# The hole between two SBUF pools, 160 bytes in place of 192

## Chip, cores and metric

One core of a Trainium2 chip runs the kernel. The metric is the device time of one execution in microseconds, the median over runs.

## What is computed

Three stages follow each other: a linear attention with decay (retention), a gated feed-forward layer (SiLU) with RMS norm, and a second layer whose activation is a softmax times its input with a layer norm. All is float32.

```python
for t in range(S):                        # S = 768, 4 batches, 8 heads of 64
    state = gamma * state + einsum('bhd,bhe->bhde', k[:, :, t], v[:, :, t])
    y[:, :, t] = scale * einsum('bhd,bhde->bhe', q[:, :, t], state)

xn = x / rms * rms_g                      # x: 3072 tokens x 512
g = xn @ w_gate; val = xn @ w_val         # 512 x 1536 each
x2 = (g * sigmoid(g) * val) @ w_out       # 1536 x 512

h = x2 @ w_in                             # 512 x 1024
e = exp(h - max(h)); sm = e / (sum(e) + 1e-9)
solu = h * sm
out = ((solu - mean) / sqrt(var + 1e-6) * g_ln) @ w_out2   # 1024 x 512
```

## The kernel before

The 3072 tokens are six blocks of 512. The weights come as 64-bit words and are turned to float32 on the way in. Every float32 product is three TensorE matmuls: both factors are split into a high and a low part (split, line 99: ACT copies the high part to float32r, VectorE or GpSimd subtracts it for the low part), and mm3 (lines 805 to 808) adds high times high, high times low, low times high into one PSUM bank. A matmul has a moving operand (rhs, at most 128x512 here) and weights (lhsT, 128x128), which TensorE loads by an instruction of its own ahead of each matmul. In the profile the name at the left of a pair is the moving operand: X<-r,wo streams r past weights from wo.

bc_block(n) walks the twelve slices m of the inner dimension (1536 = 12 x 128). Each step has a burst into bank GB (gate) and one into VB (value), twelve matmuls with xnh and xnl streaming past a weight tile w, and a burst of twelve into X0 to X3, where the gated product (r, its two parts) streams past the tile wo of the step before. In block 0 the weights are made from the raw input. Tiles of even slices are then w4 and wo (profile names w and wo), tiles of odd slices lie in CV. All are stored to DRAM (scr) and loaded again for later blocks. Blocks 2 to 5 run the second layer by de_quarters: seven products of half matrices in place of eight, at line 1180, each six matmuls of 128x512, for two halves t, with w2ih, w2il, xnh, xnl or T1 (a w4 tile) streaming past parts in r and x; then e_mm, where w2oh and w2ol stream past the transposed r. Blocks 0 and 1 use d_mm and e_mm alone, with x as weights and w2ih, w2il streaming. Block 5 runs the gate and value products in the seven-product form too, on 256 columns (seven_mm, line 913; profile line 918), with B11, B21, B22 in xnh and xnl and T1 to T4 in tiles rq, rk, kd and qd.

Between these bursts stand pieces of the attention for the next block (64 and 128 columns, lines 119 and 180) and transposes (line 1048). Their places are set by slot numbers that are written out by hand (slot, w_slot, at). Loads go through SyncE's queue in program order, stores of weights and results through ACT's.

SBUF holds two pools. A pool lays its tiles one behind the other, a tag with several buffers taking as many places, in the order in which the tags first occur; the second pool begins where the first ends. spacer(n, name) allocates n bytes in a partition that nothing uses, in the first pool; gap(name, n) does it in the second. In bytes of a partition, the built program has:

| tiles | pool | starts, modulo 512 |
|---|---|---|
| QK and w2ih, KV and w2il, xT, xnh, xnl, U, ssq, w2oh, CV and w2ol | cp, first | 448 |
| mtab 32, qtab 32, ones 192, ident 224, smaller tables elsewhere | cp | as said |
| x2 (x), r2 (r), f4 (f), st, sq, w4 (w), wo, rv, A | wp, second | 480 |
| rq, rk, kd, qd, first sm | wp, behind a gap | 384 |

The first pool begins at 16,512; the spacer of 320 bytes at line 64 puts QK at 16,832 = 32 x 512 + 448, and all large tiles behind it are multiples of 512 bytes long. The last tile of the first pool ends at 121,120; the spacer of 192 bytes at line 1321 puts the second pool's first tile, x2, at 121,312 = 236 x 512 + 480. A gap of 416 bytes ahead of rq and another ahead of kd leave these at 384, one of 96 bytes ahead of rv and one of 352 ahead of A bring these to 480 again.

Of the kernel before, what the change touches and what calls it, by code (L numbers as in the profile page):

```python
# [42 lines left out]
def retention_moe_kernel(ctx: ExitStack, tc: tile.TileContext, qk0, q2, kt, kv, wpk, w2i, w2o,  # L43
# [17 lines left out]
    def spacer(n, name):  # L61
        cp.tile([P, n // 4], F32, tag=name, name=name)
# [1255 lines left out]
    make_identity(nc, ident)  # L1318
    mhalf = cp.tile([P, 16], F32, tag="mhalf", name="mhalf")
    nc.gpsimd.memset(mhalf, -0.5)  # L1320
    spacer(192, "sp1")
    nc.gpsimd.memset(U0, 0.0)
    for t in U:
        nc.gpsimd.memset(t, 0.0)
# [192 lines left out]
```

## Time and profile before

| | |
|---|---|
| median of 3 runs | 995.77 us (995.46 to 1001.24) |
| profiled execution | 997.89 us, its span 996.1 us |
| granted TensorE clock, mean over the span | 0.99 |
| TensorE busy, matmuls | 973.9 us, 98% |
| VectorE, ScalarE, GpSimd busy | 517.4, 408.4, 449.3 us |
| DMA | 231.95 MB, 233 GB/s in the mean |

How to read it: the busy time of TensorE counts a matmul from its start to a modelled end, and successive matmuls overlap, so that 128x512 matmuls that start about 230 ns apart each last about 395 ns. A stretch can be 100% busy and yet have shorter or longer steps in it. The step, from one start to the next, is read from the timeline, in which neighbours of the same line and names are merged (x2, x6) and others stand on rows of their own.

### The profile page before, as it was taken

How to read it: one execution, taken by the hardware profiler on the slowest of the kernel's cores; microseconds unless marked ns; L12 is line 12 of the kernel's file. 1: busy time of each engine (PE TensorE's matmuls, PEld its weight loads, DVE VectorE, ACT ScalarE, POOL GpSimd, SP SyncE). 2: the span in 40 equal slices, each digit the busy share in tenths (PEclk: the TensorE clock that was granted, in tenths of full speed). 3: DMA queues.
4: the chain of work that ended last, by engine and by line, in shares of the span. 5: the costliest groups of instructions: out<-in, count | busy, mean ns of one | idle time of the engine just before them, and what ended most of it. 6: DMA issues, size and time to landing. Idle time of an engine off the chain costs nothing.

```text
span 996.1 us, 17723 instructions
## 1 busy us (share of the span) xinstructions
PE 973.9 (98%) x6636; PEld 798.8 (80%) x6636; DVE 517.4 (52%) x1040; ACT 408.4 (41%) x792; POOL 449.3 (45%) x494
## 2 busy tenths in 40 slices
PE   7999998999999999999999999999999999999998
PEld 7877787888787887888777888778788888899987
DVE  3787765463365754334574422566422457334474
ACT  2767655583244343322355221246312246321354
POOL 5886855582043395533537424527333425300022
PEclk8799999999999999999999999999999999999999
DMA  9689998996513315989943799861688954698501
GB/s 341 215 319 391 356 308 320 344 355 220 205 53 97 96 43 171 308 270 296 317 122 115 247 356 322 279 215 57 211 319 310 331 196 138 208 329 298 190 1 43
DMA packets 101334, 231.95 MB, mean 233 GB/s; under 512 B 13184, under 2 KB 43264, under 8 KB 100224
## 3 DMA queue, kind: packets, MB, share of 16 engines
q1 hardware_dynamic: 92464, 205.64, 60.5%
q10 hardware_dynamic: 8784, 25.17, 6.5%
q8 instruction: 53, 0.87, 0.3%
q14 instruction: 33, 0.27, 0.1%
HBM read 188.82 MB, written 41.94 MB: 232 GB/s over the span
## 4 chain that ended last, share of the span: by engine, by line
PE 86%; DMA 6%; POOL 3%; ACT 2%; DVE 1%; issue 1%; SPq 1%; ACTq 0%; POOLq 0%; DVEq 0%
PE X L806 10%; PE X L807 10%; PE X L808 10%; PE GB L806 7%; PE GB L808 7%; PE GB L807 7%; PE VB L806 6%; PE VB L807 6%; PE VB L808 6%; DMA wo<-scr 3%; PE X L1180 3%; PE YB L119 2%; PE VB L918 2%; PE X L1048 2%; PE YB L918 2%; PE VB L1180 2%
## 5 line engine op out<-in xcount | busy, mean ns | idle before, releaser
L825 DVE TENSOR_TENSOR f<-VB,f 128x512 f32<-128x512 f32 x60 | 41.4, 690 | 146.5 <-PE VB L808 128.7
L807 PE MATMUL X<-r,wo 128*128 128x512 f32 x260 | 102.5, 394 | 0.0
L806 PE MATMUL X<-r,wo 128*128 128x512 f32 x260 | 98.9, 395 | 3.1 <-DMA wo<-scr 3.1
L808 PE MATMUL X<-r,wo 128*128 128x512 f32 x260 | 101.5, 390 | 0.0
L854 ACT ACTIVATE f<-GB 128x512 f32<-128x512 f32 x60 | 35.7, 595 | 148.4 <-PE GB L808 148.3
L707 POOL TENSOR_TENSOR st<-st,x 128x512 int32<-128x512 int32 x52 | 70.2, 1352 | 55.7 <-ACT x L704 13.0
L100 ACT CAST r<-f 128x512 fp32r<-128x512 f32 x72 | 44.6, 619 | 121.8 <-DVE f L825 103.4
L806 PE MATMUL GB<-xnh,w 128*128 128x512 f32 (+1 forms) x220 | 88.0, 400 | 2.5 <-ACT f L854 1.1
L807 PE MATMUL GB<-xnl,w 128*128 128x512 f32 (+1 forms) x220 | 87.6, 398 | 2.1 <-DVE xnl L101 2.0
L806 PE MATMUL VB<-xnh,w 128*128 128x512 f32 (+1 forms) x220 | 87.1, 396 | 0.0
L808 PE MATMUL GB<-xnh,w 128*128 128x512 f32 (+1 forms) x220 | 87.1, 396 | 0.0
L808 PE MATMUL VB<-xnh,w 128*128 128x512 f32 (+1 forms) x220 | 86.7, 394 | 0.2 <-POOL w L101 0.2
L807 PE MATMUL VB<-xnl,w 128*128 128x512 f32 (+1 forms) x220 | 86.6, 394 | 0.0
L101 DVE TENSOR_TENSOR r<-f,r 128x512 fp32r<-128x512 f32 x72 | 61.0, 849 | 29.3 <-ACT r L100 28.7
L602 POOL TENSOR_TENSOR x<-x 128x512 f32<-128x512 f32 x24 | 31.6, 1320 | 92.1 <-DMA x<-scr 63.0
L291 POOL TENSOR_TENSOR U<-U,u 128x256 f32<-128x256 f32 x27 | 17.4, 645 | 98.8 <-PE SB L119 59.4
L806 PEld LDWEIGHTS X<-r,wo 128*128 128x128 f32 x260 | 48.7, 188 | 14.2 <-issue 3.3
L101 POOL TENSOR_TENSOR r<-st,r 128x512 fp32r<-128x512 f32 x8 | 10.3, 1288 | 110.2 <-ACT r L100 110.2
L806 PE MATMUL X<-w2oh,r 128*128 128x512 f32 (+1 forms) x144 | 57.6, 400 | 1.3 <-ACT r L1051 0.8
L808 PEld LDWEIGHTS X<-r,wo 128*128 128x128 f32 x260 | 48.8, 188 | 10.6
L807 PEld LDWEIGHTS X<-r,wo 128*128 128x128 f32 x260 | 48.8, 188 | 10.3 <-issue 0.2
L808 PE MATMUL X<-w2oh,r 128*128 128x512 f32 (+1 forms) x144 | 56.3, 391 | 0.0
(458 smaller groups left out, 2540.2 us busy)
## 6 DMA issues: line engine op xcount, KB each, us to landing
w<-scr SPq DMA_DIRECT2D x96, 512.0 KB, 5.7
wo<-scr SPq DMA_DIRECT2D x59, 512.0 KB, 5.2
x<-in_wpk SPq DMA_DIRECT2D x36, 512.0 KB, 6.0
x<-scr SPq DMA_DIRECT2D x25, 512.0 KB, 6.3
sscr<-x SPq DMA_DIRECT2D x24, 512.0 KB, 8.3
scr<-CV ACTq DMA_DIRECT2D x18, 512.0 KB, 6.0
rv<-in_kv SPq DMA_DIRECT2D x128, 64.0 KB, 2.3
scr<-w ACTq DMA_DIRECT2D x12, 512.0 KB, 5.2
```

Of the source, the lines that this page charges most:

```text
L100: h = nc.scalar.copy(hi, src)
L101: (lo_eng or nc.vector).tensor_tensor(out=lo, in0=src, in1=hi.bitcast(F32), op=ALU.subtract)
L119: return lambda: nc.tensor.matmul(out, lhsT=lhsT, rhs=rhs, start=start, stop=stop)
L602: nc.gpsimd.tensor_tensor(out=w[:, 0, :], in0=w[:, 0, :], in1=w[:, 1, :], op=ALU.add)
L707: nc.gpsimd.tensor_tensor(out=ti, in0=ti, in1=lo, op=ALU.add)
L806: nc.tensor.matmul(ps, lhsT=lh, rhs=rh, start=start, stop=False)
L807: nc.tensor.matmul(ps, lhsT=lh, rhs=rl, start=False, stop=False)
L808: return nc.tensor.matmul(ps, lhsT=ll, rhs=rh, start=False, stop=stop)
L825: recent["dve"] = nc.vector.tensor_tensor(out=a, in0=GV[1], in1=silu[:, 0, :], op=ALU.mult)
L854: recent["act"] = nc.scalar.activation(s[:, 0, :], GV[0], AF.Silu)
L918: nc.tensor.matmul(ps, lhsT=x, rhs=y[:, k, :], start=start and k + i == 0, stop=k == 1 and i == 2, skip_group_check=True)
L1180: last["mm"] = nc.tensor.matmul(bank, lhsT=x[:, k, ts_], rhs=y[:, k, :], start=start and k + i == 0, stop=k == 1 and i == 2, skip_group_ch ...
```

## The change

The spacer at line 1321, the last thing that the first pool allocates, has 160 bytes in place of 192.

```diff
     mhalf = cp.tile([P, 16], F32, tag="mhalf", name="mhalf")
     nc.gpsimd.memset(mhalf, -0.5)
-    spacer(192, "sp1")
+    spacer(160, "sp1")
     nc.gpsimd.memset(U0, 0.0)
```

No instruction of any engine stands at another place, in the order of the built program, and none has another shape. All tiles of the second pool start 32 bytes lower: those at 480 modulo 512 are at 448 then, those at 384 at 352. The first pool's tiles stay.

## Rows read from the trace of the kernel before

**Rows 1.** The page, busy time of each engine; then the chain that ended last.

```profile
PE 973.9 (98%) x6636; PEld 798.8 (80%) x6636; DVE 517.4 (52%) x1040; ACT 408.4 (41%) x792; POOL 449.3 (45%) x494
...
PE 86%; DMA 6%; POOL 3%; ACT 2%; DVE 1%; issue 1%; SPq 1%; ACTq 0%; POOLq 0%; DVEq 0%
```

**Rows 2.** Windows: length, busy us (instructions) by engine, granted clock, DMA share, GB/s.

```profile
0.00:75.00 75.00, 66.51 (x495) 56.95 (x496) 50.29 (x77) 41.67 (x81) 56.29 (x61) 0.89 0.82 292
75.00:165.00 90.00, 86.95 (x461) 69.43 (x459) 66.20 (x103) 56.72 (x98) 61.96 (x57) 1.00 0.95 336
```

**Rows 3.** Waits of TensorE: line, who was waited for, us in all, times, longest.

```profile
PE X L806 <- DMA wo<-scr: 3.1, 2, 1.8
...
PE X L1180 <- POOL r L101: 1.2, 1, 1.2
```

**Rows 4.** Timeline of TensorE, 98 to 104 us: start, length (us), line, out<-in, shapes.

```profile
98.23 0.39 PE L807 MATMUL X<-r,wo 128*128 128x512 f32 x1
...
100.50 0.39 PE L808 MATMUL X<-r,wo 128*128 128x512 f32 x1
100.72 0.40 PE L806 MATMUL GB<-xnh,w 128*128 128x512 f32 x1
...
103.29 0.40 PE L808 MATMUL GB<-xnh,w 128*128 128x512 f32 x1
```

**Rows 5.** Timeline of TensorE, 87 to 98 us, block 0, an odd weight tile.

```profile
87.19 0.40 PE L806 MATMUL X<-r,CV 128*128 128x512 f32 x1
...
89.76 0.40 PE L808 MATMUL X<-r,CV 128*128 128x512 f32 x1
...
91.69 0.39 PE L808 MATMUL GB<-xnh,CV 128*128 128x512 f32 x1
...
92.85 0.39 PE L807 MATMUL GB<-xnl,CV 128*128 128x512 f32 x1
...
95.80 0.39 PE L808 MATMUL VB<-xnh,CV 128*128 128x512 f32 x1
```

**Rows 6.** Groups of TensorE by line and shape: count, busy us, mean ns, idle.

```profile
L807 PE MATMUL X<-r,wo 128*128 128x512 f32 x260 | 102.5, 394 | 0.0
...
L806 PE MATMUL GB<-xnh,w 128*128 128x512 f32 x212 | 85.1, 401 | 2.1 <-ACT f L854 1.1 <-ACT xnh L100 1.0
...
L806 PE MATMUL X<-w2oh,r 128*128 128x512 f32 x136 | 55.3, 407 | 1.3 <-ACT r L1051 0.8 <-ACT f L1088 0.6
...
L808 PE MATMUL GB<-w2oh,r 128*128 128x512 f32 x48 | 19.3, 403 | 0.0
...
L806 PE MATMUL X<-w2ih,x 128*128 128x512 f32 x40 | 16.0, 400 | 0.0
...
L808 PE MATMUL X<-r,CV 128*128 128x512 f32 x24 | 9.6, 399 | 0.0
...
L808 PE MATMUL VB<-w2ih,x 128*128 128x512 f32 x16 | 6.3, 396 | 0.0
```

**Rows 7.** Timeline of TensorE, last block, 128x256 matmuls, six in a row.

```profile
878.15 0.87 PE L918 MATMUL YB<-qd,A 128*128 128x256 f32 x6
878.86 0.29 PE L918 MATMUL GB<-xnh,w 128*128 128x256 f32 x1
```

**Rows 8.** The page, DMA issues: out<-in, queue, count, KB each, median us to landing.

```profile
scr<-CV ACTq DMA_DIRECT2D x18, 512.0 KB, 6.0
...
scr<-w ACTq DMA_DIRECT2D x12, 512.0 KB, 5.2
```

**Rows 9.** Chain that ended last, in order of time: start, length (us), what.

```profile
485.23 11.55 DMA wo<-scr
...
649.38 11.17 DMA wo<-scr
```

**Rows 10.** Windows of TensorE alone, around the granted clock's fall at 166 us.

```profile
163.00:166.00 3.00, 1.03 (x4) 1.00 1.01 392
...
166.30:169.70 3.40, 3.40 (x10) 0.50 1.02 411
```

## The prediction

> **What bounds the kernel now.** I read four views, in this order. The page's first part and its chain say whose work sets the end: TensorE is busy 98% of the span and the chain of work that ended last runs 86% of its way over TensorE's lines, 6% over DMA, 3% over GpSimd [rows 1]. The windows say where that does not hold: up to 75 us TensorE is busy 66.5 of 75 us, and from 75 to 165 us it is busy 87 of 90 us while the DMA engines are at 0.95 [rows 2]. After that the waits of TensorE are single events of 1 to 2 us [rows 3]. So from 165 us on, and over most of 75 to 165 us, time is the number of matmuls times the step from one matmul's start to the next. A busy time of 98% does not say that this step is as short as it can be, so the third view is the timeline of TensorE, read for starts, and the fourth the groups by line and shape, read for counts.
>
> In the timeline, look at two bursts that follow each other without a gap. From 98.23 to 100.50 us ten steps of X<-r,wo (128x512) take 2.27 us: **227.0 ns** each. From 100.72 to 103.29 us eleven steps of GB<-xnh,w, the same shape, take 2.57 us: **233.6 ns** each [rows 4]. Same clock, same columns, no wait. What differs is where the operands lie. r, x, w, wo and f are tiles of the second pool, which begin at byte 480 modulo 512; xnh, xnl, CV and w2 are tiles of the first, at 448. While r streams, the weights fetched for the next matmul come from wo: 480 and 480. While xnh streams, they come from w: 448 and 480.
>
> The trace holds both cross cases, in block 0, where odd weight tiles live in CV. X<-r,CV (480 streaming, 448 weights) makes eleven steps from 87.19 to 89.76 us: 233.6 ns. GB<-xnh,CV and VB<-xnh,CV (448 and 448) make thirteen steps from 92.85 to 95.80 us: 226.9 ns [rows 5]. So r is fast with wo and slow with CV, xnh is fast with CV and slow with w. No tile is slow by itself. **Equal start bytes: 227; 32 bytes apart, in either direction: 233.6.** The difference is 6.6 ns.
>
> **What the change does.** It shortens a hole of 192 bytes to 160. No instruction is added, removed or moved on any engine. Every tile of the second pool starts 32 bytes lower: 480 becomes 448, and the few at 384 (rq, rk, kd, qd, sm) go to 352.
>
> *Matmuls that become equal.* From the groups [rows 6], 128x512 matmuls with 448 against 480: the six groups with xnh or xnl and w, 212 each, 1,272; the three with w2oh or w2ol and r into X, 136 each, 408, and into GB, 48 each, 144; the three with w2ih or w2il and x into X, 40 each, 120, and into VB, 16 each, 48; the three X<-r,CV, 24 each, 72. Line 1180 has seven products of six matmuls for two t in four blocks, 336, all mixed but the product with T1 (48): 288. Together 2,352. At 6.6 ns that is **15.5 us**.
>
> *Matmuls that are equal already* (X<-r,wo 780, the xn,CV groups 144, T1 48) keep their operands equal, since both move, or neither. But they are not always at 227: after an interruption the first five steps are slower. From 91.69 to 92.85 us, right behind an attention piece, five steps take 1.16 us, 232.0 ns each [rows 5]. An interrupted burst of equal operands so pays 5 times 5, 25 ns. Today nearly all of the 60 bursts of line 806 to 808 into X pay it, since the burst before them is mixed. After the change that is gone (60 times 25 ns, 1.5 us gained), and instead every stretch behind an interruption pays it: some 56 attention pieces and 48 groups of transposes, about 104 times 25 ns, 2.6 us lost. Net: 15.5 + 1.5 - 2.6 = **14.4 us**.
>
> *The 128x256 matmuls* of the last block step at 118 ns, six in 0.71 us, with A and w weights alike [rows 7]; all of them are mixed today (448 or 384 against 480), so the trace has no equal case of this shape. Three of seven products become equal, 216 matmuls; T1 to T4 stay 96 bytes apart. Below, nothing; above, the whole 6.6 ns, 1.4 us. Since stretches of six or twelve lie between mixed ones and would mostly be first steps, I take 0.2 us.
>
> *What shifts without a price.* The fp32 matmuls of the attention and the transposes have 64 or 128 columns; most pairs keep their distance (rq and rk 0, rv and kd 96), qd against U goes from 64 to 96 bytes, ident against f from 256 to 224: nothing, since no row gives a sign either way. DMAs now begin at 448. Stores that begin there already (scr<-CV) land in 6.0 us, those from 480 (scr<-w) in 5.2 us [rows 8]. The CV stores lie in the busiest stretch, so I take nothing; the bound is 0.8 us a transfer. TensorE waited 3.1 us in all for weights from DMA [rows 3], so that is where a later landing would show.
>
> *What does not reach the end.* Before 75 us TensorE is not the bound: about 50 mixed matmuls lie there, 0.3 us lost. From 75 to 165 us about 200 do, 1.3 us; at a DMA share of 0.95 I count half as lost, 0.7 us. The two longest transfers on the chain, 11.55 and 11.17 us of wo<-scr [rows 9], are fixed lengths that a faster TensorE overtakes: 22.7 us at 14.4 in 830 us is 0.4 us. The waits that end on another engine or a DMA [rows 3] grow where TensorE comes early: 1.7 us, by choice; for scale, those on wo<-scr and on GpSimd's r are 3.1 and 1.2 us now, 4.3 together. What is late next is therefore wo<-scr and the chain of GpSimd's r at line 101. Sum: 14.4 + 0.2 - 0.3 - 0.7 - 0.4 - 1.7 = **11.5 us**.
>
> The profiled execution took 997.89 us, 1.8 us more than its span of 996.1; the median is 995.77, so the profiled one stands 2.1 us (0.2%) above it, and the gain is taken from the median: 995.77 - 11.5 = **984.3 us**.
>
> **Rivals.**
>
> *The fast step does not hold (0.15).* If the many interruptions keep TensorE in the first-steps pace of 232.0 ns, the gain is 1.6 ns times 2,352, 3.8 us, of which the 3.1 us above do not arrive: 995 us. Half way between that and the forecast's 14.4 us stands 9.1 - 3.1 = 6.0 us, 990 us, which I take for this case, since some bursts are long. For it: X<-r,wo bursts start slow each time. Against it: thirteen steps at 226.9 in one go [rows 5].
>
> *Nothing changes (0.11).* The steps would belong to something other than the distance of the two operands, and moving both leaves them: 995.8 us. Against it stand the crossed pairs [rows 5]; for it, that w2 against r and x is seen mixed only, over a third of the count.
> [...]
>
> *Slower, by the clock (0.04).* [...]
>
> **How the numbers follow.** The forecast has 0.70: 984.3, of itself between 980.5 (14.4 us and the 256-column bound of 1.4 us, 0.5 us lost) and 987.4 (losses twice as large, 14.6 - 6.2 = 8.4 us). The range 980.5 to 991 takes in that and the upper half of the first rival and leaves out no change, slower and the rest of the first rival, about 0.2. About 1% is what a measurement of this kernel can tell from no change, here 10 us, so 985.8 us. The forecast lies 1.5 us below that bound; I give four fifths of its 0.70 to faster, 0.57; the remainder with the first two rivals is 0.39; slower 0.04.
>
> **What would show it.** In the profile after: GB<-xnh,w and GB<-w2oh,r step at 227 ns in long bursts; X<-r,wo right behind them has no slow first steps; TensorE's waits on wo<-scr and on GpSimd's r grow by 1 to 2 us together; counts and order are the same. If the w2 groups stay at 233.6 the gain is a third smaller. If all steps are 227 and the end moves less than 8 us, the time went into waits, and the waits' view will name them. If the steps are still mixed, the cause is not the distance.

## The result

The kernel with the hole of 160 bytes takes 988.28 us (median of 8 runs, 983.88 to 992.16) against 996.77 us before (8 runs): ratio 0.9908, 95% interval 0.9881 to 0.9935, 8.5 us less. Three further comparisons in the experiments below put the same two kernels side by side: 0.9890 (0.9861 to 0.9919), 0.9903 (0.9866 to 0.9939) and 0.9888 (0.9860 to 0.9917), which are 11 to 12 us each. The profiled execution took 983.88 us, its span is 982.1.

The page after, busy times and the chain by engine, beside [rows 1]:

```profile
PE 958.7 (98%) x6636; PEld 797.5 (81%) x6636; DVE 518.8 (53%) x1040; ACT 408.7 (42%) x792; POOL 448.8 (46%) x494
...
PE 74%; POOL 7%; DMA 6%; DVE 5%; ACT 3%; issue 3%; SPq 2%; ACTq 0%; POOLq 0%; DVEq 0%
```

TensorE is busy 15.2 us less with the same 6,636 matmuls, and all other engines are busy as long as before, within 2 us. The share is 98% in both: it did not show that there was something to gain, and does not show that it was gained.

The timeline of TensorE after, block 1, the first matmul of five bursts that follow each other (start, length, line, pair):

```profile
184.52 0.39 PE L806 MATMUL X<-r,wo 128*128 128x512 f32 x1
...
187.24 0.39 PE L806 MATMUL GB<-xnh,w 128*128 128x512 f32 x1
...
189.96 0.39 PE L806 MATMUL VB<-xnh,w 128*128 128x512 f32 x1
...
192.68 0.39 PE L806 MATMUL X<-r,wo 128*128 128x512 f32 x1
...
195.40 0.39 PE L806 MATMUL GB<-xnh,w 128*128 128x512 f32 x1
```

Each burst of twelve takes 2.72 us, 226.7 ns a matmul. GB<-xnh,w, 233.6 ns in [rows 4], now has the step of X<-r,wo, and X<-r,wo directly behind VB starts at the fast step at once. The products with w2, which the trace before shows with unequal starts only, moved too. GB<-w2oh,r, first and last matmul of a burst of twelve, before and then after:

```profile
294.69 0.40 PE L806 MATMUL GB<-w2oh,r 128*128 128x512 f32 x1
...
297.26 0.40 PE L808 MATMUL GB<-w2oh,r 128*128 128x512 f32 x1
```

```profile
288.41 0.39 PE L806 MATMUL GB<-w2oh,r 128*128 128x512 f32 x1
...
290.90 0.39 PE L808 MATMUL GB<-w2oh,r 128*128 128x512 f32 x1
```

Eleven steps take 2.57 us before, 233.6 ns each, and 2.49 us after, 226.4 ns each.

The waits of TensorE after, beside [rows 3]:

```profile
PE X L806 <- DMA wo<-scr: 5.3, 2, 3.1
...
PE X L1180 <- POOL r L101: 1.0, 1, 1.0
```

The wait on wo<-scr is 5.3 us in this profile, 3.1 us in the one before. That a faster TensorE made it longer is not shown: with the slow step it is 5.5 us in run d64 and 4.3 us in run d128 below. The longer of its two events, and what the clock did behind it (timeline, then windows of TensorE alone: length, busy us, granted clock, DMA share, GB/s):

```profile
479.15 0.77 PE L806 MATMUL X<-r,wo 128*128 128x512 f32 x1 [3.08 <-DMA wo<-scr]
```

```profile
476.00:478.90 2.90, 0.06 (x5) 1.00 1.02 407
478.90:482.30 3.40, 3.15 (x8) 0.50 1.02 425
```

TensorE is idle for almost all of 476.0 to 478.9 us, then the granted clock is 0.50 for 3.4 us, in which matmuls of 128x512 step at 426 ns (five steps from 479.71 to 481.84 us). There is no such stretch at this place in the profile before, but there is a longer one in d64.

### The profile page after: what moved, and what is told of

It is laid out like the page before. It is cut to its first block, busy times and chain, and to the rows that moved or that the text cites. A ratio compares the mean times of both kernels' runs of the same rounds, so it can differ in the third digit from the quotient of the medians.

```text
span 982.1 us, 17723 instructions
## 1 busy us (share of the span) xinstructions
PE 958.7 (98%) x6636; PEld 797.5 (81%) x6636; DVE 518.8 (53%) x1040; ACT 408.7 (42%) x792; POOL 448.8 (46%) x494
## 4 chain that ended last, share of the span: by engine, by line
PE 74%; POOL 7%; DMA 6%; DVE 5%; ACT 3%; issue 3%; SPq 2%; ACTq 0%; POOLq 0%; DVEq 0%
PE X L806 9%; PE X L807 9%; PE X L808 9%; PE GB L806 6%; PE GB L808 6%; PE GB L807 6%; PE VB L806 5%; PE VB L807 5%; PE VB L808 5%; DMA wo<-scr 3%; PE X L1180 3%; PE VB L1180 2%; PE YB L119 2%; PE GB L1180 2%; PE VB L918 2%
## 5 line engine op out<-in xcount | busy, mean ns | idle before, releaser
L806 PE MATMUL GB<-xnh,w 128*128 128x512 f32 (+1 forms) x220 | 86.4, 393 | 2.3 <-ACT f L854 1.1
L808 PE MATMUL GB<-xnh,w 128*128 128x512 f32 (+1 forms) x220 | 85.7, 390 | 0.1
L806 PE MATMUL VB<-xnh,w 128*128 128x512 f32 (+1 forms) x220 | 85.6, 389 | 0.0
L808 PE MATMUL VB<-xnh,w 128*128 128x512 f32 (+1 forms) x220 | 85.1, 387 | 0.3 <-POOL w L101 0.3
L808 PEld LDWEIGHTS X<-r,wo 128*128 128x128 f32 x260 | 49.1, 189 | 10.2
```

Of the source, the lines that this page charges most:

```text
L806: nc.tensor.matmul(ps, lhsT=lh, rhs=rh, start=start, stop=False)
L808: return nc.tensor.matmul(ps, lhsT=ll, rhs=rh, start=False, stop=stop)
```

## Where the gain arises and where it is lost

The first 400 matmuls of 128x512 lie in block 0 and the weights' conversion. The one after them is the first X<-r,CV behind the seam of block 0. Its row before, after, and in a later profile of the changed kernel (run again3):

```profile
165.77 1.04 PE L806 MATMUL X<-r,CV 128*128 128x512 f32 x3
```

```profile
162.59 0.63 PE L806 MATMUL X<-r,CV 128*128 128x512 f32 x1
```

```profile
163.48 1.05 PE L806 MATMUL X<-r,CV 128*128 128x512 f32 x2
```

From there to the end of the span is 996.1 - 165.8 = 830.3 us before, 982.1 - 162.6 = 819.5 after and 981.2 - 163.5 = 817.7 us in the later profile: **10.8 and 12.6 us** less. The three microseconds ahead of this row are hardly the change's work. The first 128x512 matmul of the program starts at 48.0 us in the profile before and at 44.1 to 46.2 us in four profiles of the changed kernel; but in run d64 below, where the slow step is kept, it starts at 43.85 us. The stretches of half clock in the first 45 us lie at other places in one profile than in another (from 9.3 and 33.2 us before, from 28.3 us after); that they set this start is not shown.

Part of the 10.8 and 12.6 us is still the place of a stretch at half clock. It lies wholly behind the row before (166.3 to 169.7 us, [rows 10]) and in part ahead of it after (161.4 to 164.9 us). The 421st matmul of 128x512 stands behind that stretch in every profile, at 171.98 us before and 168.20 us after. From there to the end of the span it is 10.2 us less in the profile after, and 11.5, 11.1 and 11.7 us less in three later profiles of the changed kernel (again, again2, again3).

Ahead of 165 us the change brought nothing: the lead of the changed profile is 3.9 us at the first 128x512 matmul and 3.8 us at the 421st. Behind 165 us it grows evenly, about 0.7 us for 140 matmuls, to 9.5 us at 459 us; at the seam with the wait above it falls to 7.3 us, grows again, and is 13.4 us near the end. (These leads are differences of start times of the same matmul in the two timelines.)

## Experiments

**Both pools at 480 (eq480).** Equal starts at the other place.

```diff
-    spacer(320, "sp0")
+    spacer(352, "sp0")
...
-    spacer(192, "sp1")
+    spacer(160, "sp1")
```

> The first spacer has 352 bytes in place of 320, the second 160: both pools' large tiles start at 480 modulo 512, as the second pool's did in the kernel before, and the distance is 0 as in the changed kernel. Theory 1 (the distance between moving operand and weights sets the step): GB<-xnh,w and GB<-w2oh,r step at 227 ns, TensorE's busy time 957 to 962 us, time 984 to 992. Theory 2 (the second pool's own place counts, 448 being a multiple of 64 and 480 not, for TensorE or for DMA): steps of 233 ns as in the kernel before, time 994 to 999.

984.11 us, span 982.3; the kernel before took 995.50 us beside it. One run each, here and for the next three distances. Timeline of TensorE, first matmul of four bursts:

```profile
201.50 0.39 PE L806 MATMUL X<-r,wo 128*128 128x512 f32 x1
...
204.22 0.39 PE L806 MATMUL GB<-xnh,w 128*128 128x512 f32 x1
...
206.94 0.39 PE L806 MATMUL VB<-xnh,w 128*128 128x512 f32 x1
...
209.66 0.39 PE L806 MATMUL X<-r,wo 128*128 128x512 f32 x1
```

2.72 us a burst again, with both at 480 as with both at 448: of these two places neither counts, the distance does. A share of the DMAs in the gain by where the second pool's tiles begin is excluded with it, since here that pool lies as in the kernel before. From the 421st matmul to the end it is 10.7 us less than before.

**Distances of 64, 128 and 256 bytes (d64, d128, d256).** The two spacers have 288 and 224, 224 and 288, 96 and 416 bytes in place of 320 and 192.

> Spacers of 288 and 224 bytes: the first pool at 416, the second at 480, 64 bytes apart. If only equal start bytes modulo 512 give the fast step: 233 ns in the mixed groups, time 994 to 999. If equality modulo 64 is enough: 227 ns, 984 to 992. X<-r,wo, within one pool, keeps 227 in either case.

998.28 us, span 996.5. Timeline, four bursts:

```profile
204.56 0.39 PE L806 MATMUL GB<-xnh,w 128*128 128x512 f32 x1
...
207.36 0.39 PE L806 MATMUL VB<-xnh,w 128*128 128x512 f32 x1
...
210.16 0.39 PE L806 MATMUL X<-r,wo 128*128 128x512 f32 x1
...
212.90 0.39 PE L806 MATMUL GB<-xnh,w 128*128 128x512 f32 x1
```

Mixed bursts take 2.80 us, 233.3 ns a matmul; X<-r,wo, within one pool, 2.74 us, of which the first steps are the slow ones. One group lies between: X<-r,CV, in which the second pool's tile streams past weights of the first, steps at 230.6 ns (59 steps).

The same profile shows that the wait on wo<-scr and the fall of the clock behind it also come with the slow step (waits of TensorE from 200 to 960 us, then a window of TensorE alone):

```profile
PE X L806 <- DMA wo<-scr: 5.5, 3, 3.5
```

```profile
485.80:492.60 6.80, 6.08 (x15) 0.50 1.01 415
```

Up to this place the profile of d64 runs level with the one before, 3.6 us ahead at the 421st matmul and 3.7 us at 459 us; behind it, it is 1.4 us late.

> Spacers of 224 and 288 bytes: 352 and 480, 128 bytes apart. Equality modulo 512 alone: 233 ns, 994 to 999 us. Equality modulo 64 or 128: 227 ns, 984 to 992.

998.40 us, span 996.6. Timeline, three bursts:

```profile
208.76 0.40 PE L806 MATMUL GB<-xnh,w 128*128 128x512 f32 x1
...
211.56 0.40 PE L806 MATMUL VB<-xnh,w 128*128 128x512 f32 x1
...
214.36 0.39 PE L806 MATMUL X<-r,wo 128*128 128x512 f32 x1
```

2.80 us for mixed bursts.

> Spacers of 96 and 416 bytes: 224 and 480, 256 bytes apart. Equality modulo 512 alone: 233 ns, 994 to 999 us. Equality modulo 64, 128 or 256: 227 ns, 984 to 992.

985.16 us, span 983.4. Timeline, four bursts:

```profile
203.35 0.39 PE L806 MATMUL X<-r,wo 128*128 128x512 f32 x1
...
206.07 0.39 PE L806 MATMUL GB<-xnh,w 128*128 128x512 f32 x1
...
208.79 0.39 PE L806 MATMUL VB<-xnh,w 128*128 128x512 f32 x1
...
211.51 0.39 PE L806 MATMUL X<-r,wo 128*128 128x512 f32 x1
```

2.72 us, as with a distance of 0. So what counts, as far as these five distances show it, is the distance **modulo 256**, not 512: 0 and 256 are fast, 32, 64 and 128 are slow, in these bursts by about the same 6.6 ns. From the 421st matmul to the end d256 takes 11.5 us less than the profile before, d128 0.2 us less, and d64, with its long stretch at half clock, 4.0 us more. The modulus that the change aimed at is wider than needed.

**All pairs equal (alleq).**

```diff
-        gap("gq", 416)
+        gap("gq", 512)
...
-        gap("gr", 96)
+        gap("gr", 0)
...
-            gap("gd", 416)
+            gap("gd", 512)
...
-        gap("ga", 352)
+        gap("ga", 256)
...
     ones = cp.tile([P, P], F32, tag="ones", name="ones")
     nc.vector.memset(ones, 1.0)
+    ident = cp.tile([P, P], F32, tag="ident", name="ident")
```

(A gap of 0 allocates nothing; ident is no longer allocated further down.)

> The changed kernel with the gaps of the second pool set to 512, 0, 512 and 256 bytes, so that rq, rk, kd and qd too begin at 448 modulo 512, and with ident ahead of a small table, at 192 (448 modulo 256). All pairs of the attention, the transposes and all products of the last block are then equal modulo 256. Theory 1 (equal starts help every shape): 128x256 products with T1 to T4, now 117 ns, and the 64- and 128-column matmuls step faster by up to 6 ns, busy time of TensorE down by 2 to 4 us. Theory 2 (the gain belongs to 512 columns; at 256 equal pairs step at 120 ns, mixed ones at 117): T1 to T4 go from 117 to 120 ns, busy time up by 0.5 to 1 us.

987.62 us (one run); TensorE's busy time is 962.0 us against 958.7 to 960.8 in four profiles of the changed kernel. The last block in the changed kernel (equal products with xnh and xnl, then one with T4 in qd, mixed, six in a row; the eleven steps run from the first row's start to the second's):

```profile
879.00 0.28 PE L918 MATMUL SB<-xnl,x 128*128 128x256 f32 x1
...
880.32 0.87 PE L918 MATMUL YB<-qd,A 128*128 128x256 f32 x6
881.02 0.28 PE L918 MATMUL GB<-xnh,x 128*128 128x256 f32 x1
```

and in alleq, where the products with T2 and T3 in rq and rk are equal too:

```profile
884.93 0.88 PE L918 MATMUL GB<-rq,x 128*128 128x256 f32 x6
885.65 0.88 PE L918 MATMUL VB<-rk,x 128*128 128x256 f32 x6
886.37 0.88 PE L918 MATMUL VB<-kd,x 128*128 128x256 f32 x6
```

In these bursts of 256 columns equal pairs step at 120.0 ns (eleven steps in 1.32 us in the changed kernel, six in 0.72 in alleq), mixed ones at 116.7 (six in 0.70 us). Over all 274 steps of the products with T1 to T4 the mean is 117.8 ns in the changed kernel and 119.9 in alleq. Equal is the slower of the two there, by 2 to 3 ns. The transposes and the attention's matmuls did not move: steps of 64 columns have a mean of 15.2 ns in both, the transposes with 128 columns 112.3 and 112.4 ns. Theory 2 holds for the steps: the gain belongs to 512 columns. The busy time rose by more than its 0.5 to 1 us, but the profiles of the changed kernel differ by 2.1 us among themselves.

**The changed kernel again (again, again2, again3).**

> The changed kernel itself, for its spread and beside the next two. Its runs so far spread over 8 us, with granted clocks of 0.984 to 0.991, the kernel before over 3 us. Theory 1 (in some runs TensorE's waits on wo<-scr at the seams are followed by stretches at half clock, as at 478.9 us of its profile): median 986 to 990, lower clocks in the longer runs. Theory 2 (the spread came from single bad runs): all runs within 2 us, 983 to 986.

987.65 us (984.98 to 991.02), before 999.09 us (994.57 to 1004.18, 17 runs), ratio 0.9890. Theory 1 holds for the median, but not as it was meant: the kernel before spreads as widely, over 10 us, and its long runs too have the lower granted clock (0.986 in the longest, 0.993 in the shortest). So the spread isn't brought by the change.

> The changed kernel once more, on the chip of the run before it: the step of 227 ns and the waits on wo<-scr as before; ratio to the kernel before between 0.986 and 0.992. If the ratio falls outside, the chips differ and the runs of one chip alone can be compared.

987.00 us (984.47 to 993.34), ratio 0.9903.

> The changed kernel beside it: 986 to 989 us, ratio to the kernel before 0.986 to 0.992.

988.40 us (983.00 to 989.78), ratio 0.9888.

Take the 27 runs of the changed kernel in all four comparisons and the 45 of the kernel before in the three later ones. Those with a mean granted clock of 0.990 have medians of 986.9 us (5 runs) and 997.5 us (8 runs); at 0.991 they are 984.2 (4) and 996.4 (9). At equal clock, from 0.984 to 0.991, the difference is 10.6 to 13.1 us.

**T1's loads behind the last wo tile (tlate, tlate_r; tlate_b with 192 bytes).** At the end of blocks 2 to 4 two loads of 512 KB for T1, which are wanted later, stood ahead of the last wo tile's load in SyncE's queue.

```diff
-                extra.setdefault((n, 31), []).append(lambda n=n: t_load(0, n))
+                def t_late(n=n):
+                    with tc.issue_after(recent["wo"].ins):
+                        t_load(0, n)
+                extra.setdefault((n, 34), []).append(t_late)
```

> The changed kernel, with the two loads of T1 at the end of blocks 2 to 4 issued behind the load of the last wo tile in place of ahead of it (slot 34 in place of 31, tied to that load). Theory 1 (TensorE now waits 5.3 us for wo<-scr at two seams, and a fall of the clock follows in some runs): waits on wo<-scr under 1.5 us in all, median 979 to 983, spread under 4 us, clock not under 0.989. Theory 2 (the spread has another place, at the start): the waits fall, the median does by 3 to 5 us, the spread stays.

986.28 us (980.73 to 987.06), ratio to the kernel before 0.9864 (0.9833 to 0.9895). The waits of TensorE from 200 to 960 us, longest first:

```profile
PE X L1180 <- POOL r L101: 2.1, 1, 2.1
...
PE GB L1180 <- ACT r L100: 1.1, 1, 1.1
PE VB L806 <- DMA w<-scr: 0.6, 1, 0.6
```

The wait on wo<-scr, 5.3 us in the changed kernel's profile, is gone, but 3.8 us of others stand at the same seams instead. The wait moved more than it went, and a stretch of 3.4 us at half clock is still there, now at 650.9 us. Neither theory holds here: the spread stayed (6.3 us), against theory 1, and the median fell by 1.4 us, where theory 2 had 3 to 5.

> The same late loads of T1 with the spacer of 192 bytes, as in the kernel before. There TensorE waits 3.1 us on wo<-scr. Theory 1 (a faster TensorE runs into these loads, which the kernel before mostly covers): gain of 2 to 3 us here against 4 to 7 us with 160 bytes. Theory 2 (the order of these loads is worth the same in both): the same gain in both, within 2 us.

994.35 us (991.56 to 999.37), ratio 0.9957 (0.9933 to 0.9981). With 192 bytes the same edit brings 4.7 us of 999.1, with 160 bytes 1.4 us here and 4.2 us in the repetition. Theory 1, that it would be worth more with the faster TensorE, is not borne out; within the spread the two are the same.

> The late loads of T1 with 160 bytes once more, beside the changed kernel on one chip, since their first runs overlap (986.28 and 987.65 us). Theory 1 (the wait on wo<-scr is worth its length, 5 us): 982 to 984, 3 us or more under the changed kernel. Theory 2 (most of it comes back as waits on GpSimd's and ACT's splits at the same seams, 2.1 and 1.1 us in the first profile): 0.5 to 2.5 us under it.

984.22 us (981.52 to 990.68), ratio 0.9854 (0.9821 to 0.9887), 4.2 us under again3 on the same chip. The first pair says 1.4, this one 4.2, the size of theory 1, though the waits are those of theory 2 (2.5 us on r at line 101). Each interval of the ratio overlaps that of the changed kernel. This version has the lowest ratios of all that ran; that it is faster than the changed kernel these runs don't prove.

**GpSimd's products behind S4 (tlate2).** On top of tlate, att_prep for the next block is called behind S4's low part and tied to it.

```diff
         S4 = parts(s4, nc.gpsimd)
+        if NB - 2 > n:
+            with tc.issue_after(recent["low"].ins):
+                att_prep(NCB * (n + 2))
         slot(n, base)
```

(recent["low"] is the low part made last by split; att_scores' piece no longer calls att_prep for the next block's first chunk.)

> The late loads of T1 as in the run tlate, and the attention's two products kd and qd for the next block (GpSimd) tied behind the low part of S4 at the seam of blocks 2 and 3, since GpSimd waited there for the transfer of qd with S4's low part behind it (TensorE's wait of 2.1 us on r, line 101). Theory 1 (each wait at the seams is worth its length): waits of TensorE on r at line 101 under 0.5 us, median 983 to 986, 2 to 4 us under the changed kernel. Theory 2 (the next chain is as late, ACT's and VectorE's splits at the seam): the wait moves to ACT r or another, and the median stays within 1 us of tlate's 986.3.

997.76 us (994.38 to 999.93), ratio to the kernel before 0.9986 (0.9964 to 1.0008). The waits of TensorE, longest first:

```profile
PE GB L1183 <- DMA xnh<-t2scr: 5.6, 3, 3.0
PE X L1048 <- DVE sm L1025: 2.4, 1, 2.4
PE X L1048 <- DVE r L1052: 2.3, 1, 2.3
PE GB L808 <- DVE r L1052: 2.2, 2, 1.1
```

Neither theory: the wait on r at line 101 is gone, and four others stand there, of which the other profiles have at most 1.0 us. The granted clock is at 0.50 in four stretches of 3.4 us between 486 and 688 us, where the changed kernel's profile has one. The median is 10.8 us above the changed kernel's on the same chip (987.00 us, again2). The tie did not only move kd and qd. That the order of other engines' work changed around it would fit; which instruction began it wasn't separated.

## Why the prediction was right, point by point

- **The step.** Right, and the term that carries the result. The crossed pairs in block 0 [rows 5] said that the distance of the two operands is the cause; eq480 and d256 confirm it, d64 and d128 bound it. It was called a distance modulo 512; the runs show 256. w2 against r and x, seen mixed only, behaves as the others: its neighbouring steps have means of 232.8 to 233.5 ns before and 227.3 to 228.8 after.
- **The count and the net of 14.4 us.** Over all neighbouring 128x512 matmuls without an interruption the mean step is 232.0 ns before and 227.6 ns after; for some 3,160 such pairs this is 14.2 us. Forecast was 14.4. Sorted by place, the two small terms are there as well. In the changed kernel the first six steps behind an interruption average 229.1 to 233.3 ns, 26 ns lost for each of some 95, 2.5 us where 2.6 was forecast. Before, X<-r,wo directly behind a mixed burst lost 20 ns in its first five steps, 43 times in the trace, 0.9 us where 1.5 was forecast.
- **256 columns.** This step failed. Taken as a gain of 0.2 us, with nothing as the lower bound. The sign was wrong: equal pairs step at 120 ns where mixed ones had 118 [rows 7], 0.4 us lost for 216 matmuls. The lower bound of nothing had no row behind it; the trace has no equal pair of this shape, so a loss could not be left out.
- **Before 165 us.** Forecast that 0.6 of 1.6 us arrive. The steps there gave 0.9 us (360 steps, 230.8 to 228.2 ns in the mean), and none of it arrived. That other engines and transfers set the time there would fit the DMA share of 0.95 [rows 2]; no run separates it.
- **What is late next.** wo<-scr was named, and between the two profiles its wait grew by 2.2 us, while GpSimd's r fell by 0.2; 1.7 us was forecast. The mechanism, that the wait grows because TensorE comes earlier, is not shown: d64 and d128 wait 5.5 and 4.3 us there with the slow step. Not in the sum was the stretch behind this wait at a granted clock of 0.50: 3.4 us at a step of 426 ns in place of 226.7, by which I estimate its cost at 1.6 us. It is the only one behind 165 us in the profile after; from there to it and from its end to 982 us the granted clock is 1.00. In d64, whose longest wait on wo<-scr is 3.5 us, the stretch lasts 6.8 us, so the change alone does not bring it; what does is not shown. Slower, by the clock, which had 0.04, did not come about. Behind the 421st matmul the shorter steps are worth 13.2 us (some 2,780 steps, 232.2 to 227.4 ns), and 10.2 to 11.7 us arrive.
- **The time.** 984.3 us was forecast and 988.28 measured, in the range. At 0.9% faster it lies on the side called within 1%, to which the prediction gave 0.39, and not on the one that it gave 0.57. Of the 4.0 us, 1.0 is the base (996.77 in place of 995.77) and 3.0 the gain (8.5 in place of 11.5). The later comparisons gave gains of 11.4, 11.6 and 11.7 us between medians, with medians of 999.1, 998.6 and 1000.1 us for the kernel before; the three runs of 995.77 us stand near the short end of what it does. The size of the gain was thus about right. That it is met to 0.2 us is partly luck: the 256 columns and the stretch before 165 us each came out 0.6 us worse, a fall of the clock was not in the sum, and the runs of either kernel spread over 6 to 11 us in a comparison. That the profiled runs of the two kernels are 14.0 us apart is as little the change's size: 3 to 4 us of it come from the start.
- **Nothing changes.** By the operands' distance alone the step is 226.7 or 233.3 to 233.6 ns. Where in the chip the two operands meet is not shown, nor whether it is the weights in use or those being loaded for the next matmul.

## What to carry to other kernels

Where TensorE is busy all the time, read the step between starts, not the busy share, and compare the same shape over different pairs of tiles: here two paces of one shape at one clock, 227.0 and 233.6 ns, pointed to where the operands lie, and the crossed pairs in the trace (233.6 and 226.9 ns) said so for that shape before anything was run. For 128x512 float32r matmuls keep the streamed tiles and the weights at the same start modulo 256 bytes (226.7 ns at 0 and 256, 233.3 to 233.6 at 32, 64 and 128), which costs a spacer of a few bytes; measure narrower shapes by themselves (at 256 columns 120.0 ns equal, 116.7 mixed). A gain that is spread over thousands of matmuls is easily hidden by lumps at the seams, where a load or another engine is late (waits on wo<-scr of 3.1 to 5.5 us in all) and where the granted clock stood at 0.50 behind such a wait, for 3.4 us in the profile after and 6.8 us in d64. Such lumps differ between profiles with the same step (one fall of the clock in d64, of 6.8 us, and none there in d128), so read the gain from the steps, and between two places that lie clear of them.

## What had not been expected of the hardware

- The pace of matmuls depends on the distance of moving operand and weights, as far as tested modulo 256 bytes, and not in proportion to it: 226.7 ns at 0 and 256, 233.3 to 233.6 in long bursts at 32, 64 and 128 (128x512, float32r).
- At 128x256 equal is not the fast case: 119.9 ns equal (alleq), 117.8 at 96 bytes (the changed kernel), 118.2 at 32 (before). In d64, at 64 bytes, w2oh and w2ol past r step at 113.4 ns (47 steps).
- At 64 and 128 columns of float32 no difference was seen between the changed kernel and alleq: 15.2 ns in both at 64, 112.3 and 112.4 ns in the transposes with 128.
- The pace settles: behind an attention piece the first five equal steps took 232 ns each [rows 5], directly behind a mixed burst 228.2 to 233.7 (X<-r,wo before), and behind an equal burst none did (226.7 ns a matmul, 184.52 to 195.40 us above).
- Four profiles of the changed kernel reach the first 128x512 matmul up to 2.1 us apart (44.1 to 46.2 us), and their spans differ by 2.3 us. They are of runs of 983 to 985 us; the runs of 987 to 993 us, most of them at a lower granted clock (down to 0.984), have no profile, so where those lose their time is open.
